# Shifted V read from a scratch in DRAM that holds pairs of rows, in an attention and feed-forward block on one core

## The chip, the core and the metric

The kernel runs on one core of one Trainium2 chip. Five engines of the core work side by side, each through its own list of instructions in order: TensorE (PE, matrix products, with the loads of its stationary operand shown as PEld), VectorE (DVE), ScalarE (ACT), GpSimd (POOL) and SyncE (SP, which here only issues DMAs). Sixteen DMA engines move data between DRAM and the on-chip memory, SBUF. TensorE writes to PSUM, eight banks of 128 partitions by 512 float32. Engines and DMAs wait for one another through semaphores.

The metric is the device time of one execution in microseconds. The profile of one execution gives the span from the first instruction to the last; the time of the same execution is a little longer.

## What is computed

Sequence 2048, width 512, bfloat16. A small vector `c` gives six modulation vectors; layer norm, attention and a gated feed-forward follow. The attention has 32 heads of width 16, and each query sees eight keys, at its own position and at 2, 4, ... 14 positions before it:

```python
W, dil = (8, 2)
pos = jnp.arange(S)
off = jnp.arange(W) * dil
idx = pos[:, None] - off[None, :]
mask = idx >= 0
kg = k[:, :, idx_c, :].reshape(B, H, S, W, Dh)
vg = v[:, :, idx_c, :].reshape(B, H, S, W, Dh)
logits = jnp.einsum('bhsd,bhswd->bhsw', q, kg) * scale
logits = jnp.where(mask[None, None, :, :], logits, -1000000000.0)
attn = _softmax(logits, axis=-1)
o = jnp.einsum('bhsw,bhswd->bhsd', attn, vg)
...
h = _layernorm(x, axis=-1) * (1 + ca) + sa
x = x + ga * _A_ref(h, A_wqkv, A_wo)
h = _layernorm(x, axis=-1) * (1 + cb) + sb
x = x + gb * _B_ref(h, B_w1, B_w3, B_w2)
```

`_A_ref` projects h to q, k and v, attends as above and multiplies by `A_wo`; `_B_ref` is `(silu(h @ w1) * (h @ w3)) @ w2` with 1792 hidden columns.

## The kernel before

The sequence is cut into 16 tiles of 128 rows, numbered T. Every operation is recorded by `Program.op` or `Program.dma`; a list written out at the end of the file, `ORDER`, gives one total order of all the operations, and each engine runs its share of it in that order. A second list, `SLOTS`, gives each value its buffer or PSUM bank. So the program decides nothing at run time: an engine stands at the head of its list until what the head needs is there, and everything behind it stands too. All DMAs but one are issued by SP, in its order.

The stages, with the lines that show up in the profile:

- *First layer norm and projections.* `ln_stats` (L594 to L606) normalizes on DVE. Tiles 0 to 11 are transposed on PE (L668, L712), tiles 12 to 15 by DMA. `proj_qk` (L777) and `proj_v` (L796) multiply; ACT copies the results out of PSUM, q at L785, k at L786, V at L806 into one of six buffers, `vb`. From there V is written to a scratch in DRAM by a DMA, one row of 512 per position, 128 KB a tile (`proj_v`, L810). 16 rows of zeros stand ahead of position 0 (L444).
- *Logits.* DVE multiplies q with all eight shifted k at once into `pq` (L827). PE sums over the 16 columns of a head with the constant `E` (L836): 16 matmuls of 32 output columns a tile, four next to each other in four column groups of the array, 32 queries in each. For tile 0 a mask (`before`, L833) is added first.
- *Softmax.* `shift`, `exps`, `softmax` for two tiles at a time, or four: maximum, difference, exponential, sum, reciprocal, product (L848 to L881) on DVE and ACT. PE turns the result (`turn`, L891) so that a partition holds a query and some of the eight shifts; ACT copies it to `al` (L895).
- *Values.* `values(T, ...)`: four DMAs fetch the shifted V of a tile from the scratch into `vsh` (L904), 256 KB each, 32 queries in each: 16 pairs of neighbouring queries times 8 shifts make 128 partitions, and each partition gets two neighbouring rows, 2 KB. There are two buffers of 8 KB a partition, and a third (`vshx`) where the projection weights lie once these are done with. DVE multiplies by the weights in place (`av`, L911). PE sums over the shifts with the constant `ind` (L920), eight matmuls of 32 output columns, again in four column groups; one partition in PSUM is one query. ACT copies the sum to `oa` (L926); a DMA transposes it into `ot` (L927); PE multiplies by `wo` (L944); DVE adds the residual (L948).
- *Second layer norm and feed-forward.* `ln_sums` works with sums that L948 left; the normalized rows are turned on PE (tiles 0 to 3, L668) or by DMA and modulated by ACT (L676, L653). `ffn_unit` does two products of 128 hidden columns, G and U (L960), with `silu` (L966), a copy of U (L970) or none, and the product (L971, L974); `ffn_w2` multiplies by w2 (L1003, L991), adds the residual (L1019) and stores. The groups of tiles are 0-1, 2-3, 4-7, 8-11, 12-13, 14-15. The weights of the 14 units come in four parts, units 0-3, 4-7, 8-10 and 11-13.

What sets the order around the change. On DVE the products for logits, the softmax and `av` of the first tiles are interleaved with the first layer norm of the later ones. PE fills its time with projections until the first group, tiles 0 and 1, has been through attention and the second layer norm, and with feed-forward units after that. On SP the order near tiles 2 and 3 is: four writes of V and the loads of shifted V mixed with weight loads; then the first load of tile 5's shifted V, which waits for a buffer; then the transposes of tiles 2 and 3 with weight loads between them.

## Time and profile before

| | us |
|---|---|
| median of 3 runs (lowest, highest) | 244.95 (243.38, 245.19) |
| time of the profiled execution | 245.03 |
| its span | 243.0 |
| TensorE busy | 232.6, 96% of the span |
| VectorE busy | 169.1, 70% |
| ScalarE busy | 158.3, 65% |
| GpSimd busy | 23.0, 9% |
| DMA queue of SP: 38.04 MB in 44656 packets | 62.6% of 16 engines' time |

A row of the profile names the line of the kernel, the engine, the operation and its tiles (output, arrow, inputs; buffer numbers are left out). Matmuls are pipelined and their ends are modelled: where one kind of matmul follows itself without a stop, the distance from start to start is its price, not the printed length. TensorE ran at its full clock in the whole span (granted clock 1.00).

### The profile page before, as it was taken

The page shows a single profiled execution, that of the slowest core. Times are in us where ns is not written, and L with a number is a line of the kernel's source. Part 1 is how long each engine was busy: PE and PEld are TensorE (multiplying, and loading weights), DVE is VectorE, ACT ScalarE, POOL GpSimd, SP SyncE. Part 2 cuts the span into 40 slices and gives each one's busy share as a digit, 9 for nine tenths or more (in the row PEclk, how much of TensorE's full clock was granted, in tenths as well). Part 3 has the DMA queues.
Part 4 walks back from the last instruction along what each step waited for, and adds up shares of the span by engine and source line. Part 5 has one row for each costly group of instructions (what it writes and reads, how often), then busy time and mean ns, then how long its engine had stood idle before and what let it go on. Part 6 is the DMA issues. An engine that isn't in the chain of part 4 may idle for free.

```text
span 243.0 us, 4593 instructions
## 1 busy us (share of the span) xinstructions
PE 232.6 (96%) x1789; PEld 134.1 (55%) x1814; DVE 169.1 (70%) x295; ACT 158.3 (65%) x324; POOL 23.0 (9%) x54
## 2 busy tenths in 40 slices
PE   7899999999789999999999999999999999999995
PEld 1665454545357885654444444444655447576874
DVE  5489999999697999999999698366133213155242
ACT  4358597799788978777967798876653674321300
POOL 6421330011001100011000040110000100000000
DMA  5999899599589999699897824884020030011002
GB/s 167 288 361 265 272 298 215 134 272 275 175 196 291 256 242 245 154 214 137 251 227 195 237 65 68 194 182 99 3 65 1 3 86 0 0 46 43 3 23 65
DMA packets 44685, 38.33 MB, mean 158 GB/s; under 512 B 19560, under 2 KB 35960, under 8 KB 44664
## 3 DMA queue, kind: packets, MB, share of 16 engines
q1 hardware_dynamic: 44656, 38.04, 62.6%
q8 instruction: 14, 0.23, 0.4%
q14 instruction: 7, 0.06, 0.1%
q10 hardware_dynamic: 8, 0.00, 0.0%
HBM read 29.62 MB, written 4.21 MB: 139 GB/s over the span
## 4 chain that ended last, share of the span: by engine, by line
PE 65%; DMA 14%; SPq 7%; ACT 6%; DVE 5%; issue 2%; POOL 1%; ACTq 0%
PE pall L960 33%; PE pall L1003 14%; SPq L124 7%; PE pall L777 5%; DMA sb_wm_g<-in_w_mod_dram 4%; DMA sb_ot<-sb_oa 4%; PE pall L944 3%; DMA v_scratch_dram<-sb_v 3%; PE pall L991 3%; PE pall L796 2%; PE pall L920 2%; DMA sb_h<-sb_xn 2%; PE pall L836 2%; ACT sb_h L653 2%; ACT sb_xn L620 1%
## 5 line engine op out<-in xcount | busy, mean ns | idle before, releaser
L960 PE MATMUL pall<-sb_h,sb_w 128*128 128x256 bf16 (+1 forms) x668 | 103.0, 308 | 1.4 <-DMA sb_w<-in_B_w_dram 0.7
L960 PEld LDWEIGHTS pall<-sb_h,sb_w 128*128 128x128 bf16 x672 | 64.4, 98 | 38.0 <-ACT sb_hh L970 1.5
L966 ACT ACTIVATE sb_sg<-pall 128x256 bf16<-128x256 f32 (+1 forms) x84 | 35.0, 453 | 33.5 <-PE pall L960 25.9
L1003 PE MATMUL pall<-sb_w,sb_hh 128*128 128x512 bf16 x187 | 43.2, 379 | 0.6
L827 DVE TENSOR_TENSOR sb_pq<-sb_q,sb_kT 128x4096 bf16<-128x4096 bf16 x16 | 36.3, 2277 | 0.0
L970 ACT ACTIVATE sb_hh<-pall 128x256 bf16<-128x256 f32 (+1 forms) x56 | 26.5, 494 | 10.3 <-PE pall L960 10.3
L1003 PEld LDWEIGHTS pall<-sb_w,sb_hh 128*128 128x128 bf16 x196 | 18.9, 98 | 21.3 <-DVE sb_hh L971 0.6
L974 DVE TENSOR_TENSOR sb_hh<-sb_sg,pall 128x256 bf16<-128x256 bf16 x28 | 11.1, 418 | 26.6 <-PE pall L960 23.3
L911 DVE TENSOR_TENSOR sb_vsh<-sb_vsh,sb_al 128x4096 bf16<-128x4096 bf16 x12 | 27.4, 2286 | 2.4 <-ACT sb_al L895 1.3
L777 PE MATMUL pall<-sb_h,sb_wqkv 128*128 128x512 bf16 x107 | 25.8, 379 | 1.2 <-ACT sb_v L806 0.9
L971 DVE TENSOR_TENSOR sb_hh<-sb_sg,sb_hh 128x256 bf16<-128x256 bf16 (+1 forms) x56 | 17.9, 349 | 7.3 <-ACT sb_sg L966 4.0
L1019 DVE TENSOR_TENSOR sb_o<-pall,sb_x 128x512 bf16<-128x512 f32 (+1 forms) x18 | 11.0, 627 | 13.4 <-PE pall L1003 7.3
L626 POOL TENSOR_SCALAR sb_rs<-sb_var 128x2 f32<-128x2 f32 x8 | 4.9, 608 | 145.5 <-ACT sb_xn L620 145.5
L777 PEld LDWEIGHTS pall<-sb_h,sb_wqkv 128*128 128x128 bf16 x112 | 10.3, 98 | 12.0 <-ACT sb_v L806 1.4
L944 PE MATMUL pall<-sb_wo,sb_ot 128*128 128x512 bf16 x60 | 15.7, 379 | 0.9 <-DMA sb_ot<-sb_oa 0.5
L796 PE MATMUL pall<-sb_wqkv,sb_h 128*128 128x512 bf16 x61 | 15.9, 379 | 0.3 <-issue 0.2
L653 ACT ACTIVATE sb_h<-sb_h,sb_modc 128x512 bf16<-128x512 bf16 (+1 forms) x20 | 13.2, 721 | 3.9 <-DMA sb_h<-sb_xn 3.9
L948 DVE SCALAR_TENSOR_TENSOR sb_x<-pall,sb_x 128x512 bf16<-128x512 f32 x16 | 10.9, 688 | 6.5 <-PE pall L944 6.5
L631 ACT ACTIVATE sb_xn<-sb_x,sb_nb,sb_rs 128x512 bf16<-128x512 bf16 x16 | 12.6, 808 | 4.1 <-DVE sb_nb L628 4.1
L620 ACT ACTIVATE sb_xn<-sb_x,sb_nm 128x512 bf16<-128x512 bf16 x16 | 11.5, 720 | 2.9 <-DVE sb_nm L616 2.7
L785 ACT ACTIVATE sb_q<-pall 128x512 bf16<-128x512 f32 x16 | 9.3, 604 | 4.4 <-PE pall L777 4.4
L594 DVE BATCH_NORM_STATS2 sb_st<-sb_x 128x6 f32<-128x512 bf16 x15 | 9.9, 676 | 2.7 <-DMA sb_x<-in_A_x_dram 2.7
(112 smaller groups left out, 236.1 us busy)
## 6 DMA issues: line engine op xcount, KB each, us to landing
sb_vsh<-v_scratch_dram SPq DMA_DIRECT2D x48, 256.0 KB, 4.9
sb_vshx<-v_scratch_dram SPq DMA_DIRECT2D x16, 256.0 KB, 4.0
sb_w<-in_B_w_dram SPq DMA_DIRECT2D x6, 512.0 KB, 7.8
sb_w<-in_B_w_dram SPq DMA_DIRECT2D x6, 384.0 KB, 4.4
v_scratch_dram<-sb_v SPq DMA_DIRECT2D x16, 128.0 KB, 4.3
out_dram<-sb_o SPq DMA_DIRECT2D x14, 128.0 KB, 2.0
sb_x<-in_A_x_dram SPq DMA_DIRECT2D x3, 512.0 KB, 9.8
sb_wqkv<-in_A_wqkv_dram SPq DMA_DIRECT2D x2, 512.0 KB, 7.9
```

The lines of the kernel that those rows point to most:

```text
L124: return e.dma_start(a, b, transpose=True) if transpose else e.dma_start(a, b)
L653: return e.activation(vh.at[:, ft, 0:n * P], vh.at[:, ft, 0:n * P], ACT.Identity, bias=modc[:, 8 * which + ft:8 * which + ft + 1], scale=m ...
L777: ins = e.matmul(bank(vp)[:, 0:n], wqkv[:, t, kind * D + ft * P:kind * D + (ft + 1) * P], vh.at[:, t, 0:n], start=(t == ORDER[0]), stop=(t ...
L796: ins = e.matmul(bank(vp), vh.at[:, t, tt * P:(tt + 1) * P], wqkv[:, t, 2 * D:3 * D], start=(t == ORDER[0]), stop=(t == ORDER[-1]))
L827: return e.tensor_tensor(vp.at[:], in0, in1, ALU.mult)
L911: return e.tensor_tensor(v_w, v_w, a_w, ALU.mult)
L944: ins = e.matmul(bank(vy), vt.at[:, ft, :], wo[:, ft, :], start=(ft == 0), stop=(ft == KT - 1))
L960: ins = e.matmul(bank(vp)[:, 0:n], wt[:, t, fi * P:(fi + 1) * P], vh.at[:, t, 0:n], start=(t == 0), stop=(t == KT - 1))
L966: p.op("act", lambda e: e.activation(vt.at[:, 0:n], bank(vgp)[:, 0:n], ACT.Silu), c_act(n), k, r=[vgp], w=[vt], table="silu")
L970: p.op("act", lambda e: e.activation(vh_.at[:, 0:n], bank(vup)[:, 0:n], ACT.Copy), c_act(n), k, r=[vup], w=[vh_])
L971: p.op("dve", lambda e: e.tensor_tensor(vh_.at[:, 0:n], vt.at[:, 0:n], vh_.at[:, 0:n], ALU.mult), 60 + n * 69 // 128, k, r=[vt], w=[vh_], ...
L1003: ins = e.matmul(bank(vz), vhh[fi].at[:, tt * P:(tt + 1) * P], w2[:, fi, :], start=(fi == 0), stop=(fi == NF - 1))
```

## The change

V in the scratch. A row of the scratch is now two rows of V side by side, 2 KB: row r holds V at r-2 and at r. Each tile's write puts every row of V in two places (256 KB in pieces of 1 KB), and the zero rows are 18 pairs. The first tile's write waits for the zero rows, since the two now touch the same rows of the scratch.

Loads of shifted V. A partition now stands for a query and one of four pairs of shifts, so 32 queries times 4 pairs make 128 partitions. Tiles 6 to 15 still have four loads of 32 queries and 2 KB a partition. Tiles 0 to 5 (`EARLY`) have one load of all 128 queries: a partition gets four neighbouring rows of the scratch, 8 KB in one piece. In these tiles the four column groups of PE hold queries 0, 4, 8, ..., then 1, 5, 9, ... and so on, no longer 32 neighbours each; the logits' operand is read with a step of four elements there, and with a step of one in the other tiles (two before). The mask of tile 0 has four parts, one for each column group, and lies in memory where w2 comes later.

The sum of tiles 0 to 5. No DMA transpose: PE turns the sum with four transposes into a PSUM bank, and ACT copies it from there to `ot`, which also puts the queries back in order. Tiles 6 to 15 keep the transpose by DMA. `ind` is smaller; the number and size of the matmuls that sum over shifts are the same.

`ORDER` and `SLOTS` are new lists for all operations. Read out by operation, what differs most in them:

- *PE.* First logits in the order 2, 0, 1, 3 (before: 0, 1, 3, 2), later, and in pairs next to each other. Around the first feed-forward: sum 3 and 2 and logits 6 and 7, one G group, turn 3, one G group, turn 2, one V projection, `wo` 3 and 2 (before: sum 2, logits 6, 7, sum 3, G and U of unit 7, one k projection, ..., `wo` 2, ..., `wo` 3). Units 11 to 13 of tiles 0 and 1 come after sum 5 and sum 4 (before: among the first). Tiles 14 and 15 have their logits before tiles 12 and 13, and sum 14 comes before the third group's w2 products (before: after them).
- *SP.* 142 DMAs (before: 166). The zero rows are issued after one part of `wo` (before: two parts of `wo` and a part of w3). Then two parts of w1, V writes 0 and 1, the two loads for tiles 0 and 1; V write 2, the four transposes of tiles 12 to 15, V writes 3 and 6, the loads for tiles 2 and 3, V writes 5, 4, 10, 7 and 8 with four weight loads among and after them, the loads for tiles 5 and 4, two weight loads (w1 and w3 of units 11 to 13), the loads for tiles 7 and 6.
- *DVE, ACT.* The same operations but for the six new copies on ACT; the order within the stages differs.
- *GpSimd.* `ind` and the mask come after the first layer norm's powers (before: partly ahead of them); the mask has four selects instead of one.

The diff, cut to its core (the lists left out):

```diff
-PACKET = {T: 95 if T < 2 else 122 for T in range(16)}
+WL = 4
+TB = W // DIL
+EARLY = frozenset((0,1,2,3,4,5))
+PACKET = {T: 352 if T in EARLY else 92 for T in range(16)}
...
-    ind = sb([P, 2, 16, 2], bf, "ind")
-    before = sb([P, W, 2, 16], bf, "before")
+    ind = sb([P, P // WL], bf, "ind")
...
+    NBEF = TB if 0 in EARLY else 1
+    before = (sb([P, 1, W, P // WL], bf, "before") if NBEF == 1
+              else nc.alloc_sbuf_tensor_at("sb_before", [P, TB, W, P // WL], bf, offset=nc.lookup_mloc(w2).addr))
-    v_dram = nc.dram_tensor("v_scratch_dram", (PAD + S, D), bf)
+    v_dram = nc.dram_tensor("v_scratch_dram", (PAD + S + DIL, 2 * D), bf)
...
-        p.dma(v_dram[PAD + T * P:PAD + (T + 1) * P, :], lambda: vt.at[:], k, (128, 1024), r=[vt], w=[vd], cost=400, store=True)
+        p.dma(bass.AP(v_dram, (PAD + T * P) * 2 * D + D, [[2 * D, P], [3 * D, 2], [1, D]]), lambda: bass.AP(vt.at, 0, [[D, P], [0, 2], [1, D]]), k,
+              (256, 1024), r=[vt] + ([vvpad] if T == 0 else []), w=[vd], cost=400, store=True)
...
-                if T == 0:
-                    e.matmul(PALL[0:32, c0:c0 + W * 32], ones[:, 0:32], before[:], start=True, stop=False, tile_position=(0, 0))
+                for q in range(NBEF if T == 0 else 0):
+                    e.matmul(PALL[32 * q:32 * q + 32, c0:c0 + W * 32], ones[:, 0:32], before[:, q], start=True, stop=False,
+                             tile_position=(0, 32 * q))
                 for ft in range(KT):
                     for q in range(4):
-                        ins = e.matmul(PALL[32 * q:32 * q + 32, c0:c0 + W * 32], E_sb[:, ft, :], bass.AP(vp.at, ft * P + 32 * q, [[W * KT * P, P], [KT * P, W], [1, 2], [2, 16]]),
-                                       start=(ft == 0 and (T > 0 or q > 0)), stop=(ft == KT - 1), tile_position=(0, 32 * q))
+                        cols = [q, [TB, 32]] if T in EARLY else [32 * q, [1, 32]]
+                        ins = e.matmul(PALL[32 * q:32 * q + 32, c0:c0 + W * 32], E_sb[:, ft, :],
+                                       bass.AP(vp.at, ft * P + cols[0], [[W * KT * P, P], [KT * P, W]] + cols[1:]),
+                                       start=(ft == 0 and (T > 0 or q >= NBEF)), stop=(ft == KT - 1), tile_position=(0, 32 * q))
...
-                    ins = e.transpose(at[:, :, y, :], bass.AP(ve.at[0], i * W * 32 + y * 16 * W, [[2 * W * 32, P], [1, P]]), ident[:])
+                    ins = e.transpose(at[:, :, 1 - y, :], bass.AP(ve.at[0], i * W * 32 + y, [[2 * W * 32, P], [2, P]]), ident[:])
...
-        for q in range(4):
+        near = [vv_dram[T]] + ([vv_dram[T - 1]] if T else [vvpad])
+        row = 2 * D * (PAD + T * P)
+        early = T in EARLY
+        if early:
+            p.dma(lambda: vv.at[:], bass.AP(v_dram, row, [[TB * 2 * D, P // WL], [-DIL * 4 * D, WL], [1, TB * 2 * D]]), ("vl", T),
+                  (P, 2048), r=near, w=[vv], cost=640, again=PACKET[T])
+        for q in range(0 if early else 4):
             p.dma(lambda q=q: vv.at[:, 2 * q:2 * q + 2, :],
-                  bass.AP(v_dram, (PAD + T * P + 32 * q) * D, [[2 * D, 16], [-DIL * D, W], [1, 2 * D]]), ("vl", T), (128, 2048),
-                  r=[vv_dram[T]] + ([vv_dram[T - 1]] if T else [vvpad]), part=[vv], group=loads, cost=640, again=PACKET[T])
+                  bass.AP(v_dram, row + 32 * q * 2 * D, [[2 * D, P // WL], [-DIL * 4 * D, WL], [1, 2 * D]]), ("vl", T), (P, 2048),
+                  r=near, part=[vv], group=loads, cost=640, again=PACKET[T])
...
+        if early:
+            vq = Val("ps_oT", psum)
+
+            def turn(e):
+                b = bank(vq).bitcast(bf)
+                for ft in range(KT):
+                    ins = e.transpose(b[:, ft * P:(ft + 1) * P], va.at[:, ft * P:(ft + 1) * P], ident[:])
                 return ins
...
+            p.op("pe", turn, 228, ("ot", T), r=[va, vident], w=[vq])
+            p.op("act", lambda e: e.activation(vt.at[:].rearrange("p k (t q) -> p k t q", q=TB),
+                                               bank(vq).bitcast(bf)[:, 0:KT * P].rearrange("p (k q t) -> p k t q", k=KT, q=TB), ACT.Copy),
+                 c_act(512), ("ot", T), r=[vq], w=[vt])
+        else:
             p.dma(lambda: vt.at[:], lambda: va.at[:], ("ac", T), (128, 1024), r=[va], w=[vt], cost=1250, transpose=True)
```

`PACKET`, `cost` and the like only fed the program that wrote `ORDER`; nothing of them runs.

55 lines of the change are left out of this document (22 added, 33 removed), and 127 rows, old and new, of tables (ORDER, SLOTS).

## The prediction

> **What bounds the kernel now.** I read the page's busy times first, then busy times by stretch, then the TensorE timeline where it loses time, and last who is late there.
>
> ```profile
> PE 232.6 (96%) x1789; PEld 134.1 (55%) x1814; DVE 169.1 (70%) x295; ACT 158.3 (65%) x324; POOL 23.0 (9%) x54
> ```
> ```profile
> core 0: us, PE busy (x) PEld busy (x) DVE busy (x) ACT busy (x) POOL busy (x), PEclk, DMA share, GB/s
> 0.00:20.00 20.00, 17.53 (x143) 9.74 (x144) 13.12 (x43) 9.65 (x20) 8.76 (x30) 1.00 0.88 279
> 20.00:60.00 40.00, 38.96 (x363) 20.69 (x370) 39.81 (x57) 32.62 (x61) 5.04 (x10) 1.00 0.91 241
> 60.00:75.00 15.00, 12.52 (x117) 7.04 (x116) 11.89 (x13) 11.46 (x25) 0.00 (x0) 1.00 0.73 206
> 75.00:160.00 85.00, 83.72 (x658) 47.17 (x666) 74.10 (x122) 68.80 (x144) 8.30 (x12) 1.00 0.87 194
> 160.00:240.00 80.00, 79.63 (x515) 49.45 (x519) 29.54 (x63) 35.77 (x77) 0.93 (x2) 1.00 0.17 43
> ```
> TensorE (PE) is the bound: at full clock (1.00) it is busy all but 0.4 us of 160 to 240, all but 1.3 of 75 to 160 and all but 1.0 of 20 to 60. The change touches no projection and no feed-forward matmul, so it can win only idle time of PE, and most of that lies in 60 to 75, with 2.5 us. VectorE (DVE) is full from 20 to 60 (39.81 of 40): there it paces the attention tiles that PE waits for next. The DMA engines are busy for 0.73 to 0.91 of the time up to 160.
>
> The PE timeline of that stretch (start, length, what; in brackets the idle time ahead and what ended it). A start tells more than an end, because each printed matmul drains behind the next one's start.
>
> ```profile
> 60.31 1.03 PE L777 MATMUL pall<-sb_h,sb_wqkv 128*128 128x512 bf16 x4
> 61.17 1.03 PE L796 MATMUL pall<-sb_wqkv,sb_h 128*128 128x512 bf16 x4
> 63.06 1.04 PE L777 MATMUL pall<-sb_h,sb_wqkv 128*128 128x512 bf16 x4 [0.86 <-ACT sb_v L806]
> 64.52 0.61 PE L920 MATMUL pall<-sb_vsh,sb_ind 128*32 128x512 bf16 x8 [0.42 <-ACT sb_q L785]
> ...
> 70.43 0.60 PE L960 MATMUL pall<-sb_h,sb_w 128*128 128x256 bf16 x4
> 71.77 1.49 PE L960 MATMUL pall<-sb_h,sb_w 128*128 128x256 bf16 x12 [0.75 <-DMA sb_w<-in_B_w_dram]
> 73.09 0.39 PE L891 MATMUL pall<-sb_ident,sb_attn 128*128 128x128 bf16 x4
> 73.84 1.04 PE L944 MATMUL pall<-sb_wo,sb_ot 128*128 128x512 bf16 x4 [0.36 <-DMA sb_ot<-sb_oa]
> ```
> Four 512-column matmuls take 0.86 us start to start (60.31 to 61.17). So the group at 61.17 is through at 62.03, and the next starts at 63.06: 1.03 lost. That one is through at 63.92, the next starts at 64.52: 0.60. Four matmuls of half the columns take half, 0.43: 70.86 against 71.77 is 0.91. Four transposes take a quarter, 0.22: 73.31 against 73.84 is 0.53. Together 3.1 us.
>
> Who was late, from the chain of waits, the ACT timeline and the SyncE (SP) timeline:
>
> ```profile
> 54.39 7.94 DMA v_scratch_dram<-sb_v
> ```
> ```profile
> 62.41 0.60 ACT L806 ACTIVATE sb_v<-pall 128x512 bf16<-128x512 f32 x1 [2.11 <-DMA v_scratch_dram<-sb_v]
> ```
> ```profile
> 52.54 1.81 SPq L124 DMA_DIRECT2D sb_vsh<-v_scratch_dram  x3
> ...
> 66.38 1.22 SPq L124 DMA_TRANSPOSE sb_ot<-sb_oa  x1
> 67.64 0.58 SPq L124 DMA_DIRECT2D sb_w<-in_B_w_dram  x1
> ```
> The first two stalls are one cause. A write of V, issued behind three loads of shifted V, took 7.94 us; the V buffer came free late; ScalarE (ACT), which runs in order, stood 2.11 us on it with PE's banks to empty queued behind. The third is a weight load that stood on SP behind a transpose. The fourth is the transpose by DMA itself.
>
> **The change, part by part.** The prices first: the chain of waits, the page's groups, the page's DMA issues (KB each, median us to landing).
>
> ```profile
> 31.38 0.67 PE pall L668 x12
> ```
> ```profile
> 42.97 0.55 PE pall L920 x8
> 43.51 0.88 PE pall L836 x32
> 44.39 0.43 PE pall L920 x8
> 44.82 0.16 issue
> ```
> ```profile
> L806 ACT ACTIVATE sb_v<-pall 128x512 bf16<-128x512 f32 x16 | 9.6, 606 | 2.9 <-DMA v_scratch_dram<-sb_v 2.1 <-PE pall L796 0.8
> L926 ACT ACTIVATE sb_oa<-pall 128x512 bf16<-128x512 f32 x16 | 9.5, 600 | 2.5 <-PE pall L920 2.4
> L895 ACT ACTIVATE sb_al<-pall 128x512 bf16<-128x512 bf16 x8 | 4.8, 604 | 0.3 <-PE pall L891 0.3
> ```
> ```profile
> sb_vsh<-v_scratch_dram SPq DMA_DIRECT2D x48, 256.0 KB, 4.9
> v_scratch_dram<-sb_v SPq DMA_DIRECT2D x16, 128.0 KB, 4.3
> sb_wm_s<-in_w_mod_dram SPq DMA_DIRECT2D x1, 1024.0 KB, 6.4
> sb_ot<-sb_oa SPq DMA_TRANSPOSE x16, 3.5
> v_scratch_dram<-sb_zrow SPq DMA_DIRECT2D x1, 16.0 KB, 6.6
> ```
>
> *Turning tiles 0 to 5 on TensorE.* Adds 6 x 4 transposes. Twelve take 0.67 us, 56 ns each, so 24 are 1.3 us, all of it on the path, since PE is the bound: +1.3. Adds six copies on ACT at 0.60 (L895, also bf16 from a bank): 3.6 us, four of them before 75. In 20 to 75 ACT is idle for 10.9 us (7.38 and 3.54), which covers them. The copy's pattern reads its bank in steps of 64 bytes; L806 has such a step and takes 606 against 600 for the straight L926, so I charge nothing for it. [...]
>
> The new hand-off is sum, ACT copy, turn, ACT copy, output projection. In the new PE order a projection of 0.86 or some 0.43 us feed-forward groups stand between sum and turn and between turn and projection: 1.3 us and more for copies of 0.60. That covers it unless ACT's queue is late (rival C). Removed are six transposes at 1.2 us each on SP and 3.5 us to landing, and with them the 0.53 us stall.
>
> *V as pairs of rows.* Each V write doubles to 256 KB; a 256 KB transfer lands in 4.9 where 128 KB takes 4.3, so 0.6 later each, hidden while a V buffer is free. Against that, in the new SP order the writes of tiles 5, 4, 10, 7 and 8 follow two loads of shifted V, with nothing but weights among them, and all ten writes whose buffers the last V copies need stand ahead of the next load that must wait for a shifted-V buffer. So the 2.11 us wait should go. Six tiles need one load instead of four: 18 issues fewer at 0.6. Landing: a 1 MB load took 6.4; four of 256 KB need 3 x 0.6 + 4.9 = 6.7. I take no difference. The bounds, from the landings of the present loads and from DVE's first use:
>
> ```profile
> DMA to landing us min/median/max: 3.2/4.9/8.4
> ```
> ```profile
> 38.76 2.28 DVE L911 TENSOR_TENSOR sb_vsh<-sb_vsh,sb_al 128x4096 bf16<-128x4096 bf16 x1
> ```
> A landing in 3.2 would be 3.5 us sooner, which DVE, full anyway, can't use; one in 8.4, 2 us later, is no wait for tiles 0 and 1 either. The 32 by 4 loads move the same bytes in packets of the same size: nothing taken, gain possible.
>
> *A new wait.* Tile 0's V write waits for the zero rows, 6.6 us to landing. SP issues these two weight loads earlier than now, and queued behind on SP are loads and tile 1's write; tile 0's and 1's shifted V would come about 2 us later, but DVE first needs it at 38.76. It doesn't wait for it there now, and is full up to there, which is the cover. With that cover gone it would be 2 us.
>
> *Logits.* The same 16 matmuls a tile; tile 0 has three more for the mask, side by side in four column groups: under 0.1. The operand steps by 8 bytes in tiles 0 to 5 (4 now) and by 2 in the others. Four quarters of 256 columns start in 0.11 (0.88 / 8). Doubling six tiles would cost 6 x 0.44 = 2.6 (rival D); a gain of the straight ones is bounded by nothing shown, so I take 0. [...]
>
> *GpSimd.* The mask takes four selects instead of one and a fill four times as long. It and the constants are due at the first mask and logits matmuls:
>
> ```profile
> 22.78 0.27 PE L833 MATMUL pall<-sb_before,sb_ones 128*32 128x256 bf16 x1 [0.26 <-DVE sb_pq L827]
> ```
> Were GpSimd's 8.76 us of the first 20 half as long again, it would still be idle for 6: nothing on the path.
>
> *The new order.* Runs of 32-column matmuls go from 13 to 11, by my count of both orders. Entering a run costs 0.12 (0.55 against 0.43 for the same work), leaving it 0.16: two runs less are -0.5, give or take 0.3. Feed-forward units 11 to 13, whose weights came late, move behind tile 4's sum: the 0.91 goes. The DVE work ahead of tiles 2 and 3's sums is the same set as now, so the first feed-forward can't start much before it does now, only without holes:
>
> ```profile
> 66.46 1.05 PE L960 MATMUL pall<-sb_h,sb_w 128*128 128x256 bf16 x8
> ```
> Of the 3.1 us I take the last two stalls whole (1.4) and half of the first two (0.8 of 1.6), since ACT gets 2.4 us of copies where it won 2.1: -2.2, bounds -3.1 and 0. Later:
>
> ```profile
> 118.99 5.23 PE L960 MATMUL pall<-sb_h,sb_w 128*128 128x512 bf16 x23 [0.49 <-ACT sb_h L653]
> ```
> Here PE waits for tiles 4 to 7. Their transposes by DMA now share the engines with fewer others: -0.3, bounds -1.3 (all the idle time of 75 to 160) and +1.5 (a wait of the size of the ones above, placed elsewhere by the new order). The order of the last 80 us changes little that PE would wait for: 0.
>
> **Sum.** The profiled execution took 245.03 us, 2.03 above its span; the median of the three is 244.95, so the two stand for each other. 245.0 + 1.3 - 2.2 - 0.5 - 0.3 = 243.3 us.
>
> **Rivals.** *A, all the waits go:* -3.1, -1.3, and 0.5 of the 1.0 us idle in 20 to 60, with +1.3 and -0.5: 240.9. For it: each cause is named and removed. Against it: DVE is full ahead of it and nothing makes DVE faster.
>
> *B, the waits stay:* the doubled writes hold the V buffers as long as now. Then +1.3 - 0.5: 245.8. For it: DMA is busy 0.91 of 20 to 60. Against: fewer loads ahead of them.
>
> *C, slower, ACT becomes the bound at the start of the feed-forward:* in 60 to 75 ACT is busy 11.46 of 15; without the 2.11 it stood on V, 1.43 us are left. Two new copies (1.2) land in that stretch, two just ahead of it. If PE's banks are emptied late, the turns wait for the first copy, the projections for the second, and PE waits for both. The point: ACT more than 1.43 us behind at 60. Then the 2.4 us of copies come on top of waits that stay: 245.0 + 2.4 + 1.3 - 0.5 = 248.2.
>
> *D, the 8-byte step halves the rate:* 243.3 + 2.6 = 245.9.
>
> That the change doesn't do what it says I set aside: it is a layout and an order, both written out.
>
> **Chances.** Forecast 0.40, A 0.27, B 0.13, C 0.15, D 0.05. One per cent, 2.4 us, is about what can be told from no change (three runs spread over 1.8). Faster by over that is below 242.5: most of A (0.23) and a quarter to a third of the forecast (0.12), 0.35. Slower is above 247.4: C and a little of B and D with their bounds, 0.18. Within 1%: 0.47. The range goes from just under A, 240.2, to C's price, 248.0, leaving out the low end of A and the upper half of C, under 0.2.
>
> **What would show it.** Right, if in the new profile no ACT copy of V waits on a V write by more than 0.5, PE's idle time between 60 and 75 falls from 2.5 to about 1, output projections of tiles 0 to 5 wait on no DMA, PE busy rises by about 1 and ACT by about 3.6. The first feed-forward group should start between 64 and 66. C shows as turns or projections waiting on ACT near 65; B as V writes landing in 7 us and more; D as the logits' group busy over 11 us (16 tiles now take 0.44 each by start to start). It is wrong outright if PE loses over 2 us in a place of 80 to 160 where it now runs through: then the order, not the layout, decided.

## The result: 245.93 us after 244.99, the other way than forecast

The changed kernel took 245.93 us (median of 20 runs, 244.37 to 246.98), the kernel before beside it 244.99 (20 runs, 242.79 to 245.73): ratio 1.005, 95% interval 1.0033 to 1.0067. I had forecast 243.3 with a range of 240.2 to 248.0, a small gain. It is a small loss, 0.9 us. The profiled execution took 246.02 with a span of 244.3. Here and below, ratios and their intervals leave out the few executions in a slower state, while medians and run counts take all of them.

The page of the kernel after, engines' busy times and DMA queues (packets, MB, share of 16 engines' time):

```profile
PE 236.5 (97%) x1841; PEld 137.3 (56%) x1841; DVE 169.1 (69%) x295; ACT 158.7 (65%) x328; POOL 23.1 (9%) x55
q1 hardware_dynamic: 40861, 39.37, 53.8%
q8 instruction: 14, 0.23, 0.4%
```

Busy times by stretch of the kernel after, columns as in the prediction:

```profile
20.00:60.00 40.00, 39.67 (x360) 20.05 (x359) 37.64 (x57) 31.61 (x58) 7.03 (x11) 1.00 0.83 256
60.00:75.00 15.00, 15.00 (x143) 9.21 (x142) 14.15 (x17) 14.66 (x30) 0.00 (x0) 1.00 0.75 264
75.00:160.00 85.00, 85.00 (x691) 49.59 (x690) 76.22 (x120) 67.78 (x149) 5.34 (x12) 1.00 0.69 195
160.00:240.00 80.00, 79.59 (x508) 48.56 (x506) 27.33 (x63) 36.47 (x77) 1.26 (x3) 1.00 0.13 38
```

The waits went, and more of them than I had counted on: TensorE is busy for 15.00 of 15 in 60 to 75 (before 12.52) and for 85.00 of 85 in 75 to 160 (before 83.72). The DMA queue took 53.8% of the engines' time instead of 62.6% for 1.3 MB more. And yet the time is longer. So TensorE must be doing more. Its busy time rose by 3.9 us where I had put 1.3 for the turns. (The profile of before lacks 25 matmul records, 1789 against 1814 weight loads, so a little of the 3.9 is the record.) The logits' group of the kernel before, then groups of the kernel after, show where:

```profile
L836 PE MATMUL pall<-sb_pq,sb_E 128*32 128x256 bf16 x256 | 8.9, 271 | 0.0
```
```profile
L842 PE MATMUL pall<-sb_pq,sb_E 128*32 128x256 bf16 x256 | 11.6, 324 | 0.0
L809 ACT ACTIVATE sb_v<-pall 128x512 bf16<-128x512 f32 x16 | 9.4, 599 | 1.4 <-PE pall L799 1.2
L951 ACT ACTIVATE sb_ot<-pall 128x512 bf16<-128x512 bf16 x6 | 3.5, 602 | 0.0
```

The 256 logits matmuls (line 842, line 836 before) take 11.6 us where they took 8.9. That is the sign I had named for rival D. The chain of waits of the kernel after, start, length, what, gives the price where two tiles follow each other, the first two rows with step 4, the other two with step 1:

```profile
35.94 1.95 PE pall L842 x31
54.38 1.93 PE pall L842 x31
...
82.82 0.87 PE pall L842 x32
...
118.13 0.99 PE pall L842 x32
```

Two straight tiles cost 0.87, or 0.99 with the entry into a run of 32-column matmuls in it. Two tiles with step 4 cost 1.95. That is 0.48 more a tile, 2.9 for six. I had put this term at 0.

### The profile page after: what moved, and what is told of

It reads as the page before. It is cut to its first block, busy times and chain, and to the rows that moved or that the text cites. A ratio compares the mean times of both kernels' runs of the same rounds, so it can differ in the third digit from the quotient of the medians.

```text
span 244.3 us, 4644 instructions
## 1 busy us (share of the span) xinstructions
PE 236.5 (97%) x1841; PEld 137.3 (56%) x1841; DVE 169.1 (69%) x295; ACT 158.7 (65%) x328; POOL 23.1 (9%) x55
## 3 DMA queue, kind: packets, MB, share of 16 engines
q1 hardware_dynamic: 40861, 39.37, 53.8%
## 4 chain that ended last, share of the span: by engine, by line
PE 87%; DMA 6%; ACT 4%; SPq 2%; issue 0%; DVE 0%; DVEq 0%; ACTq 0%
PE pall L976 39%; PE pall L1019 15%; PE pall L780 10%; PE pall L960 6%; PE pall L799 5%; PE pall L842 4%; PE pall L934 3%; DMA sb_wm_s<-in_w_mod_dram 3%; SPq L124 2%; DMA sb_h<-sb_xn 2%; PE pall L1007 2%; ACT sb_h L679 1%; DMA out_dram<-sb_o 1%; ACT sb_h L656 1%; PE pall L900 1%; PE pall L744 1%
## 5 line engine op out<-in xcount | busy, mean ns | idle before, releaser
L982 ACT ACTIVATE sb_sg<-pall 128x256 bf16<-128x256 f32 (+1 forms) x84 | 36.3, 457 | 33.1 <-PE pall L976 30.2
L1019 PE MATMUL pall<-sb_w,sb_hh 128*128 128x512 bf16 x196 | 44.3, 379 | 0.0
L986 ACT ACTIVATE sb_hh<-pall 128x256 bf16<-128x256 f32 (+1 forms) x56 | 26.6, 502 | 11.6 <-PE pall L976 11.4
L926 DVE TENSOR_TENSOR sb_vsh<-sb_vsh,sb_al 128x4096 bf16<-128x4096 bf16 x13 | 29.4, 2282 | 0.5 <-ACT sb_al L904 0.5
L987 DVE TENSOR_TENSOR sb_hh<-sb_sg,sb_hh 128x256 bf16<-128x256 bf16 (+1 forms) x56 | 17.7, 349 | 15.2 <-ACT sb_hh L986 11.3
L780 PE MATMUL pall<-sb_h,sb_wqkv 128*128 128x512 bf16 x112 | 26.5, 379 | 0.0
L1035 DVE TENSOR_TENSOR sb_o<-pall,sb_x 128x512 bf16<-128x512 f32 (+1 forms) x18 | 11.1, 626 | 11.3 <-PE pall L1019 8.2
L799 PE MATMUL pall<-sb_wqkv,sb_h 128*128 128x512 bf16 x64 | 16.6, 379 | 0.3 <-ACT sb_h L679 0.3
L629 POOL TENSOR_SCALAR sb_rs<-sb_var 128x2 f32<-128x2 f32 x8 | 2.1, 263 | 145.1 <-ACT sb_xn L623 145.1
L940 ACT ACTIVATE sb_oa<-pall 128x512 bf16<-128x512 f32 x16 | 9.3, 610 | 4.9 <-PE pall L934 4.7
L842 PE MATMUL pall<-sb_pq,sb_E 128*32 128x256 bf16 x256 | 11.6, 324 | 0.0
```

Of the source, the lines that this page charges most:

```text
L780: ins = e.matmul(bank(vp)[:, 0:n], wqkv[:, t, kind * D + ft * P:kind * D + (ft + 1) * P], vh.at[:, t, 0:n], start=(t == ORDER[0]), stop=(t ...
L799: ins = e.matmul(bank(vp), vh.at[:, t, tt * P:(tt + 1) * P], wqkv[:, t, 2 * D:3 * D], start=(t == ORDER[0]), stop=(t == ORDER[-1]))
L842: ins = e.matmul(PALL[32 * q:32 * q + 32, c0:c0 + W * 32], E_sb[:, ft, :], bass.AP(vp.at, ft * P + cols[0], [[W * KT * P, P], [KT * P, W]] ...
L926: return e.tensor_tensor(v_w, v_w, a_w, ALU.mult)
L982: p.op("act", lambda e: e.activation(vt.at[:, 0:n], bank(vgp)[:, 0:n], ACT.Silu), c_act(n), k, r=[vgp], w=[vt], table="silu")
L986: p.op("act", lambda e: e.activation(vh_.at[:, 0:n], bank(vup)[:, 0:n], ACT.Copy), c_act(n), k, r=[vup], w=[vh_])
```

## The experiments

Theory S: the 8-byte step of the logits' operand halves TensorE's rate, and these 2.9 us ate what the removed waits gave. The rivals are named in the expectations, each with its numbers. A ratio is always to the kernel before, measured beside the kernel in question.

### Four kernels about the step

*Step by step.* The kernel after, with another step in each early tile and in tile 6:

```diff
-                        cols = [q, [TB, 32]] if T in EARLY else [32 * q, [1, 32]]
+                        cols = ([q, [TB, 32]] if T in (0, 6) else [64 * (q // 2) + q % 2, [2, 32]] if T in (1, 7) else [q, [3, 32]] if T == 2
+                                else [2 * q, [1, 2], [8, 16]] if T == 4 else [2 * q, [8, 16], [1, 2]] if T == 5 else [32 * q, [1, 32]])
```

> The kernel after with other steps in the logits' moving operand, tile by tile: step 4 (8 bytes) in tiles 0 and 6, step 2 in 1 and 7, step 3 in 2, step 1 in 3, neighbours inside and 16-byte jumps outside in 5, the reverse (16-byte jumps inside) in 4. The queries come mixed up in these tiles, so their logits stand in other places than they should; the work is the same. Theory S (the 8-byte step itself halves TensorE's rate, wherever it stands): start to start, four quarters of 256 columns take 0.11 us with step 1 and 2, 0.21 with step 4, in tile 0 and in tile 6 alike; step 3 between these or at one of them; the 16-byte step inside about 0.4. Rival K (the logits of tiles 0 to 5 are slow because of the time at which they run, beside loads with 8 KB a partition): tiles 0 to 5 take 0.21 whatever the step, 6 and 7 take 0.11.

The kernel took 244.87 us (one run). Its TensorE timeline (logits are line 843; the tiles are 2, then 0, then 1 and 3, 4 and 5, 6, 7):

```profile
28.82 0.93 PE L843 MATMUL pall<-sb_pq,sb_E 128*32 128x256 bf16 x16
...
34.94 1.07 PE L843 MATMUL pall<-sb_pq,sb_E 128*32 128x256 bf16 x32
...
52.43 2.90 PE L843 MATMUL pall<-sb_pq,sb_E 128*32 128x256 bf16 x32
...
65.53 1.08 PE L843 MATMUL pall<-sb_pq,sb_E 128*32 128x256 bf16 x16
...
66.87 0.61 PE L843 MATMUL pall<-sb_pq,sb_E 128*32 128x256 bf16 x16
```

From start to start, four quarters of 256 columns took, by the single records:

| step of the operand | tile | ns |
|---|---|---|
| 1 (2 bytes) | 3, and 8 to 15 | 109 |
| 2 (4 bytes) | 1, 7 | 111 to 115 |
| 3 (6 bytes) | 2 | 175 |
| 4 (8 bytes) | 0, 6 | 221, 222 |
| pairs of neighbours, 16 bytes apart | 5 | 227 |
| 16 bytes at every element | 4 | 445 |

Tile 6 runs late, beside 2 KB loads, and is as slow with step 4 as tile 0. Tiles 1 and 3 run early and are fast with step 2 and 1. So it is the step and not the time or the traffic (rival K falls). The step alone counts, and evenly. One price fits the table, my estimate from it: each 16 bytes of a partition (a line, from here on) that the operand passes over cost no less than four columns' time (1.7 ns, 4 x 109 / 256). With four elements of a line used, or eight, the columns take that long anyway (111 to 115 and 109 ns); with two or one they don't (221 and 445), and the line sets the price. Worked out this way, step 3 would take 164 ns, step 4 218 and 16 bytes at every element 436, each a little under what was measured (175, 221 and 445).

*Step 1 in the kernel after, and step 4 in the kernel before.* Each is one line (of the second, the access pattern alone is shown):

```diff
 (after)
-                        cols = [q, [TB, 32]] if T in EARLY else [32 * q, [1, 32]]
+                        cols = [32 * q, [1, 32]]
 (before)
-bass.AP(vp.at, ft * P + 32 * q, [[W * KT * P, P], [KT * P, W], [1, 2], [2, 16]])
+bass.AP(vp.at, ft * P + (q if T < 6 else 32 * q), [[W * KT * P, P], [KT * P, W]] + ([[4, 32]] if T < 6 else [[1, 2], [2, 16]]))
```

> The kernel after with step 1 instead of 4 in the logits of tiles 0 to 5; each column group then gets 32 neighbouring queries, and the logits of these six tiles stand in other places than they should. Same matmuls, same order. Theory S: 16 matmuls of a tile fall from 0.97 to 0.44 us, six tiles give 3.1 us back, nearly all on TensorE's path: 242.8 us, 0.987 of the kernel before (245.0), the last matmul 3 us sooner. Rival N (the time went into the turns and the new order, the slow logits lie in time that TensorE would have waited anyway): 245 to 246, no change against the kernel after.

> The kernel before with step 4 in the logits of tiles 0 to 5 and nothing else; the logits of these tiles stand in other places than they should. Theory S: six tiles lose 0.53 us each, 3.1 us; the kernel before has some 3 us of waits between 20 and 75 that may swallow a part, so +2 to +3.1: 247 to 248, ratio 1.008 to 1.013. Rival N: under +0.7 us, ratio below 1.003.

Step 1 in the kernel after: 243.63 us (12 runs), ratio 0.9955, interval 0.9925 to 0.9986. Against the kernel after's ratio of 1.005 that is 2.3 us back. The chain of waits of this kernel has the pairs at the same places:

```profile
33.58 0.99 PE pall L842 x32
51.04 0.99 PE pall L842 x32
```

0.99 instead of 1.95 and 1.93: the mechanism is what S says. But the time gave 2.3 where the matmuls gave 2.9. The two intervals alone allow anything from 1.5 to 3.2, so the times don't show that something is missing; the profiles do, and that is the subject of the next four kernels.

Step 4 in the kernel before: 246.75 us (6 runs), ratio 1.0087, interval 1.0058 to 1.0116, so 2.1 us more from one access pattern. In its chain the pair that took 0.88 takes

```profile
43.88 1.86 PE pall L836 x29
```

and the rest of the 2.9 can lie in the waits that this kernel has between 60 and 75 (TensorE busy 13.98 there instead of 12.52); the interval, 1.4 to 2.8 us, nearly reaches 2.9. Rival N, that the slow logits lie in idle time, falls in both.

*A version with the same V scratch and a step of 2.* If a partition takes two neighbouring rows (4 KB) instead of four, a column group gets every second query of half a tile:

```diff
-            p.dma(lambda: vv.at[:], bass.AP(v_dram, row, [[TB * 2 * D, P // WL], [-DIL * 4 * D, WL], [1, TB * 2 * D]]), ("vl", T),
-                  (P, 2048), r=near, w=[vv], cost=640, again=PACKET[T])
+            for j in range(2):
+                o = p.dma(lambda j=j: vv.at[:, 4 * j:4 * j + 4, :],
+                          bass.AP(v_dram, row + 64 * j * 2 * D, [[2 * 2 * D, P // WL], [-DIL * 4 * D, WL], [1, 2 * 2 * D]]), ("vl", T),
+                          (P, 2048), r=near, part=[vv], group=loads, cost=640, again=PACKET[T])
...
-                        cols = [q, [TB, 32]] if T in EARLY else [32 * q, [1, 32]]
+                        cols = [64 * (q // 2) + q % 2, [2, 32]] if T in EARLY else [32 * q, [1, 32]]
```

The mask and the copy that puts the queries back in order follow; the second load stands right behind the first.

> The kernel after with two loads instead of one in tiles 0 to 5, each of 64 queries with two neighbouring rows of the scratch, 4 KB a partition. A column group then holds every second query of one half of the tile, so the logits' operand steps by two elements (as before the change), the mask and the copy that puts the queries in order follow, and all else stays. Theory S: the 3.1 us of the slow logits go; six more DMA issues of 0.6 us on the SyncE queue are hidden: 242.8 us, ratio 0.987 to 0.993 against the kernel before. Rival N: 245 to 246. Rival L (the single load of 8 KB a partition is what took the waits at 60 to 75 away): the waits come back, over 1 us of TensorE's idle time in 60 to 75, and the time stays above 244.

243.13 us (12 runs), ratio 0.9931, interval 0.9903 to 0.9958: faster than both kernels, and 2.9 us below the kernel after by the ratios. TensorE is busy for 15.00 of 15 in 60 to 75, so rival L falls: the waits don't hang on the 8 KB load.

### Four kernels about the missing part

In the profiles of the step-1 kernel and of the kernel with two loads of 4 KB a partition (the two-load kernel from here on) TensorE waits at a place where it did not wait before the change or in the profile after. The TensorE timeline of the two-load kernel:

```profile
166.57 1.04 PE L967 MATMUL pall<-sb_wo,sb_ot 128*128 128x512 bf16 x4
168.83 2.36 PE L983 MATMUL pall<-sb_h,sb_w 128*128 128x256 bf16 x20 [1.23 <-ACT sb_sg L989]
```

ACT is named, but the chain of waits leads back to a transpose:

```profile
160.35 0.59 SPq L125
160.99 5.21 DMA sb_h<-sb_xn
166.22 2.08 ACT sb_h L658 x4
```

The second transpose of tiles 14 and 15 (`h` of the second layer norm) took 5.21 us; ACT stood on it with PE's banks to empty behind. The DMA view of the half microsecond from 163.5 shows who else was there (packets, MB, share):

```profile
q1 hardware_dynamic: 381, 0.10, 83.4%
q8 instruction: 1, 0.02, 18.1%
```

One packet of 16 KB on the queue for instructions, a code load of 1.4 us in the trace, among the 4 to 256 byte packets of the transposes. There are 14 such loads in the span of the kernel after. TensorE has 1841 matmuls and as many weight loads, 3682 instructions, and 3682 / 14 is about 260 for one load, an estimate that puts all 14 down to TensorE. TensorE's own work doesn't wait for them in 75 to 160, where five of the 14 lie and it is busy for 85.00 of 85. What a load does to the transposes beside it, the kernels below show.

Theory C of the expectations says this: a code load among the packets of the second transpose makes it land late, and TensorE waits for it; where the code load lies differs from one execution to the next.

The first two kernels are the kernel after and the two-load kernel, unchanged. The third moves one issue; the fourth doubles the turns, `for ft in 2 * list(range(KT))`:

```diff
+ORDER.insert(ORDER.index(607) + 1, ORDER.pop(ORDER.index(609)))
```

> The kernel after, unchanged, beside the next three on one chip. Step 1 in the logits gave back 2.3 us where the start-to-start times of the logits say 3.1. Theory C: the rest goes into a wait at 165, where in the profile of the step-1 kernel a code load stood among the packets of the second transposes of tiles 14 and 15 and PE lost 1.1 us; that wait comes or not by the execution. Then this kernel is at 245.9 and 2.0 to 2.8 us above the two-load kernel, and its logits take 0.97 a tile again. Rival M: the 2.3 was the spread of runs, the difference is 3.1 or more. The first modulation product starts between 11.4 and 12.7 in executions of either kernel if the head's lateness is the execution and not the change.

> The two-load kernel (64 queries and 4 KB a partition in each load, step 2), unchanged, on the same chip as the kernel after. 242.7 to 243.7; 2.0 to 2.8 us below the kernel after by theory C, 3.1 by rival M. In the profile the wait ahead of the feed-forward at 165 to 168 is there (1 us or more) where the code load falls within 3 us behind the issue of the second transpose, and gone where it falls later.

> The two-load kernel with one issue moved: the last load of shifted V for tile 15 ahead of the first of the two transposes of tiles 14 and 15, instead of between them. The second transpose is issued 0.6 us sooner. Theory C (PE waits there for that transpose): 0.3 to 0.7 us less wait at 165 to 168, 242.6. Rival: the code load's place decides alone, no change against the two-load kernel (within 0.4).

> The two-load kernel with the four transposes of each early tile done twice into the same bank: 24 more transposes. If TensorE is the bound at each of the six places, 24 x 56 ns = 1.3 us more than the two-load kernel, 244.5. Rival: two or three of the turns stand in time that PE would wait anyway, then 0.7 or less.

| | us (runs) | ratio, interval |
|---|---|---|
| after, again | 246.03 (12) | 1.0054, 1.0027 to 1.0082 |
| two loads, again | 243.46 (12) | 0.9936, 0.9907 to 0.9965 |
| two loads, one issue moved | 242.53 (9) | 0.9909, 0.9878 to 0.9940 |
| two loads, turns twice | 243.23 (12) | 0.9934, 0.9907 to 0.9961 |

After minus two loads is 2.6 us by the medians and 2.9 by the ratios, give or take 0.7 to 1.0: that doesn't tell the 2.0 to 2.8 of theory C from the 3.1 of rival M. The second profile of the two-load kernel is as C said: the code load comes later, and the wait is gone. The moved issue gained 0.9 by the medians and 0.7 by the ratios, the upper end of what C expected or above it. Doubling the turns cost nothing, against the 1.3 of the plain sum; the rival (0.7 or less, the turns stand in waits) allows that. But it does cost TensorE its time; the chain of waits of the turn-twice kernel has

```profile
65.48 0.45 PE pall L954 x8
66.36 0.45 PE pall L954 x8
```

where the two-load kernel has

```profile
65.34 0.22 PE pall L954 x4
66.00 0.22 PE pall L954 x4
```

So something else must have become shorter by as much. The 48 further instructions (24 matmuls and their weight loads) move the code loads behind them: the one that lay at 163.0 in the two-load kernel's second profile lies at 157.3. Over the profiles up to here, this is the code load near the second transpose, in us behind the transpose's issue, and the time that TensorE then lost at 165 to 170, both by the single records:

| profile | code load behind the issue | lost |
|---|---|---|
| step 1 | 2.5 | 1.1 |
| two loads | 2.6 | 1.4 |
| after, again | 2.6 | 0.7 |
| after | 3.2 | 0 |
| step by step | 3.2 | 0 |
| two loads, again | 3.2 | 0 |
| two loads, issue moved | 3.4 | 0 |
| turns twice | ahead of it | 0 |

At up to 2.6 it falls among the transpose's packets, from 3.2 on these are through. (The profile after pays elsewhere: there the code load at 209.0 lies 2.1 us behind the issue of the second transpose of the next pair, which lands late, and TensorE loses 0.6 us at 213.4 to 214.1. Its chain of waits:

```profile
206.89 4.53 DMA sb_h<-sb_xn
...
214.11 5.85 PE pall L976 x52
```

So both profiles of the kernel after have such a wait, one at each place.) For the second transpose at 160 to 164, the issues' landing (KB where known, median us) says the same, first the two-load kernel, then its second profile:

```profile
sb_h<-sb_xn SPq DMA_TRANSPOSE x1, 5.2
```
```profile
sb_h<-sb_xn SPq DMA_TRANSPOSE x1, 3.1
```

### Four kernels to settle it

The first asks whether the price of the step belongs to the four column groups, in `proj_qk` and in the loop of the logits:

```diff
+        step = {(1, 0): 4, (1, 1): 2, (2, 0): 8, (3, 0): 16}.get((gi, kind), 1)
...
-                    ins = e.matmul(bank(vp)[:, 0:n], wqkv[:, t, kind * D + ft * P:kind * D + (ft + 1) * P], vh.at[:, t, 0:n],
+                    ins = e.matmul(bank(vp)[:, 0:n], wqkv[:, t, kind * D + ft * P:kind * D + (ft + 1) * P],
+                                   bass.AP(vh.at, t * 512, [[KT * 512, P], [1, step], [step, n // step]]),
...
-                for ft in range(KT):
-                    for q in range(4):
-                        cols = [q, [TB, 32]] if T in EARLY else [32 * q, [1, 32]]
+                pairs_ = [(ft, q) for ft in range(KT) for q in range(4)] if T not in (6, 7) else [(ft, q) for q in range(4) for ft in range(KT)]
+                if pairs_:
+                    for ft, q in pairs_:
+                        cols = [q, [TB, 32]] if T in EARLY or T == 6 else [32 * q, [1, 32]]
```

The second has both the moved issue and the turns twice. The third takes the two-load kernel and splits the first eight warm-up products:

```diff
-            def mm(e, vw=vw):
-                return e.matmul(bank(vw), ones[:, 0:P], ones[:], start=True, stop=True)
+            def mm(e, vw=vw, split=4 if warmed[0] < 8 else 1):
+                for s in range(split):
+                    n = 512 // split
+                    ins = e.matmul(bank(vw)[:, s * n:(s + 1) * n], ones[:, 0:P], ones[:, 0:n], start=True, stop=True)
+                return ins
```

The fourth is the kernel with the moved issue, unchanged.

> The kernel after with two probes; queries and keys come mixed up in the tiles named. First, the projections with the whole array (128 by 128) read their moving operand with other steps, 512 columns each as before: q of tiles 4 to 7 step 4, k of tiles 4 to 7 step 2, q of tiles 8 to 11 step 8, q of tiles 12 to 15 step 16. Second, the logits of tiles 6 and 7 do the four matmuls of one column group one behind the other instead of going round the four groups, tile 6 with step 4, tile 7 with step 1. Theory P (the four column groups share one read of 16 bytes of each partition a cycle, so 4 bytes a stream; one stream alone has all 16): steps 2, 4 and 8 cost nothing with the whole array, 216 ns a matmul from start to start, step 16 costs double, 432; tile 6 takes as long as tile 7 from the first start to the last. Rival Q (an 8-byte step halves the rate of any moving operand): step 4 takes 432 and step 8 864 ns with the whole array, and tile 6 twice tile 7.

> The kernel with the moved issue (two loads, last load of tile 15 ahead of both transposes) and the transposes of the six early tiles done twice. Theory C (24 transposes of 56 ns are on TensorE's path, and the turn-twice kernel before hid them only because its 48 more TensorE instructions moved the code load that had disturbed the transposes at 161 to 164): nothing is left to be won there, 242.5 + 1.3 = 243.8. Rival H (the turns stand in time that PE waits anyway): 242.5, within 0.5. In the profile the time from the first logits to the last start of TensorE shows which: 208.5 us without the second turn.

> The two-load kernel with the first eight warm-up products of 512 columns each split into four of 128: the same columns, 24 matmuls and so 48 TensorE instructions more in the head, as many as the second turns had. Theory C: every later code load comes earlier, the one near 163 moves to about 157, ahead of the transposes of tiles 14 and 15, and the wait at 165 to 168 is gone: 0.6 to 1.0 below the two-load kernel's 243.3. Rival H: nothing changes, 243.3 within 0.4.

> The kernel with the moved issue, unchanged, beside the others on one chip: 242.5 again, ratio to the kernel before 0.988 to 0.994; if the first time was the spread of the runs, 243.3.

*The whole array.* The kernel took 278.56 us (one run). Its chain of waits, four matmuls of 512 columns with step 4, 2, 8, 1 and 16:

```profile
25.12 1.80 PE pall L781 x4
...
46.48 0.90 PE pall L781 x4
...
61.31 3.60 PE pall L781 x4
...
68.45 0.86 PE pall L781 x4
...
75.87 3.67 PE pall L781 x4
```

Per matmul 450 ns with step 4, 225 with step 2, 900 with step 8, 216 with step 1, 918 with step 16. Theory P, that the column groups share a read and one stream alone would be free, falls: the price is the same 2 and 4 times with the whole array. From step 8, 16 bytes, to step 16 it hardly grows (900 and 918). Tile 6 took twice tile 7 (894 against 436 ns for its 16 matmuls), which looks like Q but proves nothing here: tile 6 ran at a granted clock of 0.50 (97.1 to 98.0 us), tile 7 at 1.00 (98.7 to 99.1). Nor does the order inside a tile show what one column group alone can do: 16 matmuls took 436 ns in either order, their starts come in fours in both, and the records don't name the column group.

*The code load.*

| | us (runs) | ratio, interval |
|---|---|---|
| issue moved and turns twice | 243.36 (12) | 0.9954, 0.9928 to 0.9980 |
| two loads, code loads shifted | 242.26 (6) | 0.9899, 0.9857 to 0.9942 |
| issue moved, again | 242.51 (6) | 0.9903, 0.9865 to 0.9941 |

With the wait out of the way the doubled turns cost 0.8 by the medians and 1.1 to 1.2 by the ratios, against 1.3 for 24 x 56 ns; rival H, that they stand in idle time, said 0. The profiles say it more sharply than the times. This is the stretch from the start of the first logits matmul to the start of TensorE's last matmul, by the single records, and the time that TensorE lost in it to transposes held up by a code load:

| profile | stretch, us | lost | without it |
|---|---|---|---|
| after; again | 211.5; 211.6 | 0.6; 0.7 | 210.9; 210.9 |
| step 1 | 209.1 | 1.1 | 208.0 |
| two loads; again | 209.8; 208.3 | 1.4; 0 | 208.4; 208.3 |
| two loads, issue moved; again | 208.6; 208.3 | 0; 0 | 208.6; 208.3 |
| two loads, code loads shifted | 208.3 | 0 | 208.3 |
| turns twice; with the issue moved | 209.4; 209.7 | 0; 0 | 209.4; 209.7 |

Step 4 against step 1 is 2.9 us, all that the matmuls say, and the second turns are some 1.2 us. In these profiles the step-1 kernel waits 0.4 to 0.5 us longer than the kernel after, which brings the 2.9 near the 2.3 above.

And 48 instructions more in the head, which do no work that was not done before, made the two-load kernel 0.8 to 0.9 us faster by the ratios. In its profile the code load lies at 156.3, ahead of the transposes, and the view of 160.9 to 166.3 has no packet on the instruction queue; the landing there:

```profile
sb_h<-sb_xn SPq DMA_TRANSPOSE x1, 3.2
```

Of the versions that do no extra work, the two-load kernel with one issue moved is the fastest: 242.53 and 242.51 us, about 1% below the kernel before in both sets of runs.

Each of these differences in time alone is near the width of its interval (0.7 to 1.0 us); together with the landings and the places of the code loads they agree. That the code load holds up the transposes shows at two further places, where the same 48 instructions work both ways. The transpose of `oa` behind the second one, issued between 160 and 165, lands in 2.4 us in the three profiles with 48 instructions more, where the code load is long gone, and in 3.6 to 4.5 in the profiles of the new order without them, where one falls 1.2 to 2.1 us behind its issue. The first transpose of the next pair, issued between 202 and 207, is the other way round: 3.8 us in those three, with a code load 1.7 us behind its issue, and 2.3 in the others, where the load comes 3.4 us behind or later. TensorE waited for none of these. How a code load holds up a transpose (which of the 16 engines, which queue) wasn't tried.

## Why the prediction was wrong, step by step

The sum with what was measured in it, beside the terms as I put them:

| term | forecast | measured | from |
|---|---|---|---|
| start | 245.0 | 245.0 | |
| 24 turns | +1.3 | +1.3 | 56 ns from start to start; doubled, 0.8 to 1.2 in time and 1.2 in the stretch |
| waits and runs (-2.2, -0.5, -0.3) | -3.0 | -4.0 | 242.4, the level of the two kernels without slow logits and without the wait at 165 to 170 (242.53 and 242.51, 242.26), is 245.0 + 1.3 - 4.0 and some 0.1 for step 2; by their ratios (0.9909, 0.9903, 0.9899) the level is 242.5 to 242.8 and the term -3.9 to -3.6; the three weren't measured apart |
| logits, step 4 | 0 | +2.9 | pairs of 1.95 and 1.93 against 0.99, the first two tiles alike; 210.9 against 208.0 in the stretch |
| order of the last 80 us | 0 | +0.7 | the remainder: 245.9 less the terms above (0.3 to 0.6 with the ratios); the waits of the two profiles of the kernel after are 0.6 and 0.7 |
| sum | 243.3 | 245.9 | |

**The step that failed is "Logits": "the same 16 matmuls a tile ... so I take 0".** I had the right bound (doubling six tiles is 2.6, rival D with 245.9), no row that spoke for either end, and gave the good end 0.95. That end was an estimate of mine which no run had shown, and no run shows the 0: the runs showed 0.48 us more a tile, 2.9 for six. Two elements of 2 bytes in a line, step 4, run at half the rate (221 against 109 ns), and so do two neighbours in every line (227); four in a line, step 2, run at nearly the full one (111 to 115). The kernel before stepped by 4 bytes, the last of the measured steps that is nearly free (step 3, 6 bytes, took 175); from its rows nothing could be seen of the next. That should have left the chance of D near even, not at 0.05, and with it the forecast of a gain would not have stood.

**Waits and runs: right in kind, too small.** All four stalls of 60 to 75 went, where I had let half of the first two stay because ACT gets new copies. The V copies wait for no write (line 809: 1.4 us idle, nearly all on PE). ACT got its six copies, 602 ns each, but its busy time rose by 0.4 and not 3.6. Most of the difference is that the new order also has fewer table loads (rows ACT_TABLE_LOAD), at the exponential (line 866, then 875) and at `silu` (line 966, then 982):

```profile
L966 ACT ACT_TABLE_LOAD x4 | 5.1, 1283 | 0.1
L866 ACT ACT_TABLE_LOAD x3 | 3.8, 1283 | 0.1
```
```profile
L982 ACT ACT_TABLE_LOAD x3 | 3.8, 1283 | 0.0
L875 ACT ACT_TABLE_LOAD x2 | 2.6, 1283 | 0.0
```

These are the groups of the kernel before and of the kernel after, one form each: two table loads of 1.28 us less, 2.6 of the 3.2 that are missing; the rest I didn't trace. I had read the order of the operations for PE and SP, and for ACT only counted them.

**Rivals.** A (all waits go, 240.9) was right about the waits of 60 to 160 and wrong about the sum, by D. B (the waits stay) ends at 245.8, next to the result, for a wrong reason: a time near a rival's is no evidence for it, TensorE's 15.00 of 15 is against it. D (the step halves the rate) had the mechanism, and its price of 2.6 for the six tiles is near the 2.9. That its sum, 245.9, is the result to the decimal is luck: the forecast under it gained 1.0 too little from the waits and lacked the 0.7 at the end. C didn't come: ACT is busy 14.66 of 15 in 60 to 75, so it was as near as I had feared, but no TensorE wait falls there. (Its price was 248.2; the range was put at 248.0.)

**What held.** The turns. The copy out of PSUM with its 64-byte step: line 951 takes 602 ns where the straight copy on line 940 took 610. The V writes twice as large, the zero rows and the mask: nothing waits on them in the profile after. What didn't hold beside the sum: the first feed-forward was forecast for 64 to 66. It starts at 68.36 in the kernel after; without the slow logits, in the two-load kernel's second profile, it starts as follows (of the 3.6 us between the two, 0.9 lie ahead of the first logits, so some 2.8 are left for the logits with step 4):

```profile
64.73 0.61 PE L983 MATMUL pall<-sb_h,sb_w 128*128 128x256 bf16 x4
```

**What I had left out.** "The order of the last 80 us changes little that PE would wait for: 0." PE does wait there in some executions, since the new order puts a load of shifted V between two transposes whose usual landing of 3.1 to 3.2 us leaves TensorE 0.5 to 0.7 us to spare (landings of 4.4, 4.8 and 5.2 cost 0.7, 1.1 and 1.4). No row of before shows when a code load comes in the new order.

**What looked like a cause and is mostly the execution.** In the profile after, the first modulation product starts 1.2 us later than in that of before, with the same issues ahead of it. TensorE timelines of the kernel after and of the step-1 kernel:

```profile
12.62 0.55 PE L508 MATMUL pall<-sb_csz,sb_wm_s 128*128 128x1 bf16 x16 [1.32 <-DMA sb_wm_s<-in_w_mod_dram]
```
```profile
11.27 0.54 PE L508 MATMUL pall<-sb_csz,sb_wm_s 128*128 128x1 bf16 x16
```

Over the 12 profiles with the new order it starts between 11.3 and 12.9, at 12.1 on average, in the kernel before at 11.43 and with step 4 in it at 11.72. So most of the 1.2 us is the execution, and one profile of each kernel would have made a cause of it; with two profiles of the old order, a part of some 0.5 us isn't ruled out.

## What to carry to other kernels

When a layout changes the step of a matmul's moving operand, count the 16-byte lines that it reads: here, with 2-byte elements, a step of two was nearly free, four halved the rate and eight quartered it, on the whole array (225, 450 and 900 ns against 216) and in column groups alike (111 to 115, 221, and 445 for jumps of 16 bytes, against 109). A term with two ends and no row for either should be a rival near even, and not a zero in the sum. Where two kernels differ by less than 1 us, compare the stretch between two fixed places of the chain in several profiles before the total: an execution's head alone moved by 1.6 us.

## What the runs showed of the hardware that I had not expected

Beside the price of a line (above): the code loads. A 16 KB packet on the queue for instructions, one for some 260 TensorE instructions by the count above, made a transpose by DMA land in 4.4 to 5.2 us instead of 3.1 to 3.2, when it fell up to 2.6 us behind the transpose's issue (the kernel with the steps of 8 has one more: 2.7 us behind, 5.1 to landing). 48 instructions added in the head, with no work of their own, went with a code load at 156.3 instead of 163.0, and took some 0.8 us off the time, near the width of the intervals.

And in the kernel with the steps of 8, TensorE's granted clock was 0.50 for a while. Busy times of 51 to 60 us, in which some step-8 matmuls and contiguous ones follow each other (granted clock third from the end):

```profile
51.00:60.00 9.00, 9.00 (x21) 2.51 (x20) 5.63 (x3) 3.40 (x7) 0.00 (x0) 0.69 0.18 60
```

The mean of 0.69 hides two states. In shorter windows the granted clock is 0.50 from 51.2 to 54.1, 1.00 from 54.2 to 57.5 and 0.50 again from 57.6 to 60.9. At 0.50 the contiguous matmuls took 427 ns instead of 216. The step-8 ones of this stretch, 878 to 900 ns, ran nearly all at 1.00, so they say little about the price of a line at the lower clock. Tile 6 says more: with step 4 its 16 matmuls took 894 ns at 0.50, and 893 at 1.00 in the step-by-step kernel. So the price of a line did not double here with the clock halved (894 against 893), where that of a column did (427 against 216).

All four stretches of 0.50 in this kernel's span that lie between matmuls begin during the last of four matmuls with step 8 or 16 (at 50.7, 57.5, 64.4 and 95.1 us), though not every such four is followed by one. Why is open. All this was seen in this one run.
